# Rows of the weights regrouped by four, chunk 0's key products cut into column halves, and the key weights split on VectorE

## The chip, the cores and the metric

The kernel runs on one core of a Trainium2 chip. TensorE (PE) multiplies matrices; its weight loads are shown apart (PEld). VectorE (DVE), ScalarE (ACT) and GpSimd (POOL) do the elementwise work, and SyncE (SP) issues most of the transfers between HBM and the core's memory (SBUF); a few are issued from ACT's queue. Matrix results land in PSUM. The metric is the device time of one execution in microseconds, as the median of several runs.

## The reference, cut to what matters

All inputs are float32: x is 2048 x 512, wq 512 x 512, wk and wv 512 x 16, w_gate and w_up 512 x 1792, w_down 1792 x 512, gate_w has 512 entries.

```python
g = _sigmoid((x * gate_w).sum(-1, keepdims=True))
# attention: 32 query heads of width 16 share one key and one value head
q = (x @ wq).reshape(B, S, 32, 16)
k = x @ wk
v = x @ wv
p = softmax(einsum(q, k) * 16 ** -0.5)
a = einsum(p, v) @ wo
# feed-forward
b = (silu(x @ w_gate) * (x @ w_up)) @ w_down
return g * a + (1 - g) * b
```

Everything that is multiplied with x sums over the 512 columns of x. In which order these 512 are summed, and in which groups of 128, leaves the result as it is, as long as x and the weights use the same order.

## The kernel before, in words

**Precision.** A product of float32 matrices is made from three products of rounded parts: each operand is split into a high part and the rest (`split`, lines 111 to 114: a cast, L113, and a subtraction, L114), and high by high, high by low and low by high are summed in PSUM.

**Layout.** The 512 columns of x are cut into KD = 4 groups of 128, one group for each of four matrix products. The weights lie in SBUF with a partition p and a group k: before, the row k * 128 + p of a weight matrix lies in partition p, group k. For x the same is made by transposing 128 x 128 squares on PE.

**The start.** The rows of x are worked on in four chunks of 512 rows, each of four tiles of 128 rows. SP fetches the rows of chunk 0 in four transfers and those of the later chunks in two each (`load_x`, L639); chunks share two buffers, so chunk 2 waits until chunk 0 has been transposed. ACT's queue fetches wk, wv and gate_w into one tile `wkv_f` (L643 to L645). `prepare_kv` splits them with eight operations on POOL (L113, L114): wkv_h and wkv_l have 113 columns, which hold the keys three times at two places, the values and the gate.

`transpose_x(c, i)` transposes two row tiles of chunk c: eight PE transposes (L689) into one of two PSUM buffers (`pss`), with the square of x as the loaded weights and the identity streamed through. For chunk 0, KEEP = 6 products of a zero matrix (`zeros`, L675) follow each row tile. Then ACT copies the buffer out as the high part (L693) and DVE subtracts to get the low part (L694), which also sets the buffer free for the next but one `transpose_x`.

`project_kv(c)` makes the 12 products of wkv with chunk c (L123; 512 columns each): eight with the high part of x, four with the low. ACT takes the result out (L709, L711), and POOL makes the rows of `ks` from it (L715, L717). `load_wq(m)` fetches 128 columns of wq (SP, L144) and splits them on POOL.

The engines work each through their own list in the order in which the code is written (`manual_schedule`); the start's order is that of the lines 740 to 786. From line 789 on, jobs for queries, gate, up and down products (L223) are woven between attention scores (L833), exponentials (L844) and value products (L860). Weights w_gate and w_up come through `load_w` and the views `wg_v` and `wu_v`.

Of the kernel before, what the change touches and what calls it, by code (L numbers as in the profile page):

```python
# [18 lines left out]
P = 128  # L19
# [3 lines left out]
DH = 16  # L23
# [19 lines left out]
LONG = 8  # L43
GAP = 36
WARM = 30
KEEP = 6
RATE = 8
FIRST = 6
PTB = 3
# [18 lines left out]
def tile_gated_mix(ctx, tc, x, wq, wk, wv, wo, w_gate, w_up, w_down, gate_w, out):  # L68
# [13 lines left out]
    x_d = dpool.tile([2, 2, P, KD, CH], F32, name="x_d")  # L82
    w_d = dpool.tile([3, NF, 2, P, D], F32, name="w_d")
    o_w = dpool.tile([KD, 2, P, D], F32, name="o_w")
    wq_v = wq.rearrange("(k p) n -> p k n", p=P)

    ident = cpool.tile([P, P], F32, name="ident")
    make_identity(nc, ident)
# [23 lines left out]
    def split(hi, lo, src, eng=nc.gpsimd, eng_hi=nc.vector):  # L112
        eng_hi.tensor_copy(hi, src)  # L113
        eng.tensor_tensor(lo, src, hi.bitcast(F32), ALU.subtract)  # L114
# [8 lines left out]
            nc.tensor.matmul(ps, a, b, start=(i == 0), stop=(i == n - 1))  # L123


    wg_v = w_gate.rearrange("(k p) f -> p k f", p=P)
    wu_v = w_up.rearrange("(k p) f -> p k f", p=P)
    W, HT = {}, {}
    ACTS, DEFER, LOADS, HOLD, EVAC, FRESH = [], [], [], [], [], set()

# [501 lines left out]
    with tc.tile_pool(name="apool", bufs=1) as ap, tc.tile_pool(name="apool2", bufs=2) as a2:  # L632
        XT = {}

        def load_x(c, n):
            XT[c] = a2.tile([P, TC, D], F32, name="xt", bufs=2)
            for i in range(0, TC, n):
                t = c * TC + i
                nc.sync.dma_start(XT[c][:, i:i + n, :], x[t * P:(t + n) * P, :].rearrange("(i p) d -> p i d", p=P))  # L639

        load_x(0, 1)
        wkv_f = ap.tile([P, KD, 2 * DH + 1], F32, name="wkv_f")
        nc.scalar.dma_start(wkv_f[:, :, 0:DH], wk.rearrange("(k p) n -> p k n", p=P))  # L643
        nc.scalar.dma_start(wkv_f[:, :, DH:2 * DH], wv.rearrange("(k p) n -> p k n", p=P))
        nc.scalar.dma_start(wkv_f[:, :, 2 * DH:], gate_w.rearrange("(k p o) -> p k o", p=P, o=1))  # L645
        load_x(1, 2)


        wkv_h = ap.tile([P, KD, KW], F32R, name="wkv_h")
        wkv_l = ap.tile([P, KD, KW], F32R, name="wkv_l")  # L650

        def prepare_kv():
            k, v, g = slice(0, DH), slice(DH, 2 * DH), slice(2 * DH, 2 * DH + 1)
            for r in (0, RT):
                to = [w[:, :, r:r + 3 * DH].rearrange("p k (i n) -> p k i n", i=3) for w in (wkv_h, wkv_l)]
                src = wkv_f[:, :, k].unsqueeze(2).to_broadcast([P, KD, 3, DH])
                split(to[0], to[1], src, nc.gpsimd, nc.gpsimd)
            for to, src in ((3 * DH, v), (KW - 1, g)):
                rows = slice(to, to + src.stop - src.start)
                split(wkv_h[:, :, rows], wkv_l[:, :, rows], wkv_f[:, :, src], nc.gpsimd, nc.gpsimd)  # L660

        spread = ap.tile([DH, DH, HG], F32, name="spread")

        def prepare_norms():
            nc.vector.tensor_reduce(sel, ident.rearrange("p (r h) -> p h r", h=HG), axis=AX.X, op=ALU.max)
            nc.vector.tensor_copy(spread, ident[:DH, :DH].unsqueeze(2).to_broadcast([DH, DH, HG]))
            nc.vector.memset(vaug[:, :, DH:], 1.0)

        nc.gpsimd.memset(ks.bitcast(F32), -1.0)
        nk = ap.tile([DH, NCH + 1], F32, name="nk")  # L670
        VZ = {}

        def zeros(n):
            for i in range(n):
                nc.tensor.matmul(pw[:, :P], warm, warm, start=True, stop=True)  # L675

        def transpose_x(c, i):
            if i == 0:
                if c < 2:
                    new_x(c)  # L680
                else:
                    XC[c] = [PAIR[1].tile([P, S], F32R, name="pt", bufs=PTL).rearrange("p (k s) -> p k s", k=KD)
                             for _ in range(2)]
            xt, (xh, xl) = XT[c], XC[c]
            pt = ps_s.tile([P, 2 * CH], F32, name="pss")
            ptv = pt.rearrange("p (k t) -> p k t", k=KD)
            for j in range(2):
                for k in range(KD):
                    nc.tensor.transpose(ptv[:, k, j * P:(j + 1) * P], xt[:, i + j, k * P:(k + 1) * P], ident)  # L689
                if c == 0:  # L690
                    zeros(KEEP)
            hi = xh[:, :, i * P:(i + 2) * P]
            nc.scalar.activation(hi, ptv, AF.Copy)  # L693
            nc.vector.tensor_tensor(xl[:, :, i * P:(i + 2) * P], ptv, hi.bitcast(F32), ALU.subtract)  # L694

        def store_x(c):
            for j, part in enumerate(XC[c]):
                nc.sync.dma_start(x_d[c - 2, j], part.bitcast(F32))

        def project_kv(c):  # L700
            cs = slice(c * CH, (c + 1) * CH)
            if c % 2 == 0:
                VZ[c // 2] = ap.tile([KW, 2 * CH], F32, name="vz", bufs=2)
            pk = ps_f.tile([P, CH], F32, name="pf")

            terms = [(w[:, k], XC[c][0][:, k]) for k in range(KD) for w in (wkv_h, wkv_l)]
            mm(pk[:KW, :], terms + [(wkv_h[:, k], XC[c][1][:, k]) for k in range(KD)])
            vz = VZ[c // 2][:, c % 2 * CH:(c % 2 + 1) * CH]
            nc.scalar.activation(vz, pk[:KW, :], AF.Copy)  # L709
            ka = a2.tile([DH, CH], F32, name="ka")  # L710
            nc.scalar.activation(ka, pk[:DH, :], AF.Abs)  # L711
            nc.vector.tensor_reduce(nk[:, c:c + 1], ka, axis=AX.X, op=ALU.max)

            for r in (0, RT):
                nc.gpsimd.tensor_copy(ks[r:r + 3 * DH, cs], vz[r:r + 3 * DH, :])  # L715
                lo = slice(r + 2 * DH, r + 3 * DH)
                nc.gpsimd.tensor_tensor(ks[lo, cs], vz[lo, :], ks[lo, cs].bitcast(F32), ALU.subtract)  # L717


        def spread_k():  # L720
            nc.vector.tensor_reduce(nk[:, NCH:], nk[:, :NCH], axis=AX.X, op=ALU.max)
            pn = ps_o.tile([P, CH], F32, name="po")
            nc.tensor.matmul(pn[:, 0:1], spread.rearrange("i r h -> i (r h)"), nk[:, NCH:], start=True, stop=True)  # L723
            nc.vector.tensor_copy(kmax, pn[:, 0:1])

        def transpose_v(b):
            pv = ps_s.tile([P, 2, CH], F32, name="pss")
            for i in range(NT // 2):
                nc.tensor.transpose(pv[:, i // TC, i % TC * KW:(i % TC + 1) * KW], VZ[b][:, i * P:(i + 1) * P],  # L729
                                    ident[:KW, :KW])  # L730
            for j in range(2):
                ts = slice(b * NT // 2 + j * TC, b * NT // 2 + (j + 1) * TC)
                pvb = pv[:, j, :TC * KW].rearrange("p (t n) -> p t n", n=KW)
                nc.vector.tensor_copy(vaug[:, ts, 0:DH], pvb[:, :, 3 * DH:RT])
                nc.scalar.activation(g_sb[:, ts], pvb[:, :, KW - 1], AF.Tanh, scale=0.5)

        with tc.manual_schedule():

            warm = ap.tile([P, P], BF16, name="warm")
            nc.vector.memset(warm, 0.0)  # L740
            pw = ps_o.tile([P, CH], F32, name="po")
            zeros(WARM)
            prepare_kv()
            load_wq(0)
            transpose_x(0, 0)
            transpose_x(0, 2)
            prepare_norms()
            load_x(2, 2)
            transpose_x(1, 0)
            transpose_x(1, 2)  # L750
            load_x(3, 2)
            new_qs(0)
            project_kv(0)
            transpose_x(2, 0)
            transpose_x(2, 2)
            project_kv(1)
            transpose_x(3, 0)
            transpose_x(3, 2)
            project_kv(2)
            store_x(2)  # L760
            transpose_v(0)
            project_kv(3)
            store_x(3)
            load_wq(1)
            load_wq(2)
            load_part()
            for c in range(NCH):
                if c == 2:
                    load_wq(3)
                job = query(0, c)  # L770
                for i in range(job.size):
                    if c == 0 and i == job.size - 1:
                        spread_k()
                    job.step(i)
                if c == 0:
                    transpose_v(1)

                    nc.vector.tensor_scalar(g_sb, g_sb, 0.5, 0.5, op0=ALU.mult, op1=ALU.add)
                    nc.vector.tensor_scalar(c_sb, g_sb, -0.5, 0.5, op0=ALU.mult, op1=ALU.add)
            for nm in "gu":  # L780
                load_w(nm, 0)
            run(STORES, NCH)
            fill(GAP)
            WIDE.append(1)
# [350 lines left out]
```

## Time and profile before

| what | value |
|---|---|
| median of 3 runs | 1311.89 us (1311.57 to 1312.14) |
| the profiled execution's own time | 1310.52 us |
| its span in the profile | 1308.7 us |
| PE busy | 1301.7 us (99%) |
| ACT, DVE, POOL busy | 1077.6, 795.0, 308.5 us |
| start of the first x transposes | 4.17 us |
| start of the first query product | 26.45 us |

Times inside a profile count from the start of the span, and the execution's own time is 1.8 us longer than the span. PE rows are pipelined: a row's duration is longer than the time to the start of the next, so the cost of one product in a stream is the distance between starts.

### The profile page before, as it was taken

What the parts mean: (1) busy time and instruction counts of PE and PEld (TensorE: products, weight loads), DVE (VectorE), ACT (ScalarE), POOL (GpSimd) and SP (SyncE); (2) the same over time, 40 slices, a digit from 0 to 9 for tenths busy, and PEclk for the clock granted to TensorE, in tenths of its full rate; (3) what the DMA queues carried; (4) which work ended last, traced back from release to release, by engine and by line L of the source; (5) the groups of instructions that cost most, each with busy time, mean ns of one, the idle gap of its engine ahead of it and who ended that gap; (6) DMA issues with size and microseconds to landing.
All of it is one profiled execution on the core that took longest, in us unless ns stands there. A gap on an engine that the chain in (4) does not pass through costs nothing.

```text
span 1308.7 us, 27220 instructions
## 1 busy us (share of the span) xinstructions
PE 1301.7 (99%) x10791; PEld 766.1 (59%) x10791; DVE 795.0 (61%) x1210; ACT 1077.6 (82%) x1626; POOL 308.5 (24%) x765
## 2 busy tenths in 40 slices
PE   9999999999999999999999999999999999999998
PEld 7655555555555555555555555555556555555586
DVE  4668665576565665666566566566566666566632
ACT  4588898888888988888889889889898888898710
POOL 7463331442252272273130000000000000001031
PEclk9999999999999999999999999999999999999999
DMA  8674221232233363354134341243242342153075
GB/s 292 210 235 136 81 57 45 67 113 61 69 108 138 127 219 113 109 181 134 62 132 157 120 144 55 71 156 110 85 141 90 119 148 61 62 181 94 25 229 200
DMA packets 104821, 161.57 MB, mean 123 GB/s; under 512 B 12144, under 2 KB 43632, under 8 KB 103024
## 3 DMA queue, kind: packets, MB, share of 16 engines
q1 hardware_dynamic: 102960, 159.56, 37.8%
q8 instruction: 88, 1.44, 0.5%
q10 hardware_dynamic: 1728, 0.20, 0.1%
q14 instruction: 45, 0.37, 0.1%
HBM read 101.52 MB, written 57.67 MB: 122 GB/s over the span
## 4 chain that ended last, share of the span: by engine, by line
PE 99%; DMA 0%; DVE 0%; SPq 0%; ACT 0%; issue 0%
PE pf L223 39%; PE po L860 35%; PE pss L833 20%; PE pf L123 4%; PE pss L689 0%; DMA xt<-in_A_x_dram 0%; PE pss L729 0%; SPq L639 0%; DVE xl L694 0%; ACT xh L693 0%; DVE ot L594 0%; PE po L723 0%; PE po L1047 0%
## 5 line engine op out<-in xcount | busy, mean ns | idle before, releaser
L844 ACT ACTIVATE pt<-pss 128x1024 f32<-128x1024 f32 (+1 forms) x1024 | 776.0, 814 | 148.0 <-PE pss L833 112.8
L839 DVE COPY pt<-pss 128x512 f32<-128x512 f32 x504 | 348.0, 691 | 389.3 <-PE pss L833 382.7
L860 PE MATMUL po<-pt,vaug 128*32 128x512 f32 x4096 | 460.0, 594 | 0.0
L833 PE MATMUL pss<-qs,ks 64*128 64x512 f32 x2048 | 412.7, 406 | 0.0
L833 PEld LDWEIGHTS pss<-qs,ks 64*128 64x128 f32 x2048 | 200.3, 183 | 197.3 <-ACT pt L844 97.1
L860 PEld LDWEIGHTS po<-pt,vaug 128*32 128x32 f32 x4096 | 126.9, 109 | 268.6 <-issue 261.2
L844 ACT ACTIVATE pt<-pt 128x512 f32<-128x512 f32 x504 | 281.4, 629 | 0.0
L223 PE MATMUL pf<-xh,wgh 64*128 64x512 f32 x444 | 161.3, 391 | 0.0
L223 PE MATMUL pf<-xl,wgh 64*128 64x512 f32 x444 | 161.3, 391 | 0.0
L223 PE MATMUL pf<-xh,wgl 64*128 64x512 f32 x444 | 160.5, 391 | 0.0
L223 PE MATMUL pf<-xl,wuh 64*128 64x512 f32 (+1 forms) x444 | 159.5, 391 | 0.0
L223 PE MATMUL pf<-xh,wuh 64*128 64x512 f32 (+1 forms) x444 | 159.4, 392 | 0.0
L223 PE MATMUL pf<-xh,wul 64*128 64x512 f32 (+1 forms) x444 | 158.0, 391 | 0.0
L223 PE MATMUL pf<-wdl,hh 64*128 64x512 f32 (+1 forms) x411 | 143.4, 390 | 0.0
L223 PE MATMUL pf<-wdh,hh 64*128 64x512 f32 (+1 forms) x411 | 143.0, 390 | 0.0
L223 PE MATMUL pf<-wdh,hl 64*128 64x512 f32 (+1 forms) x411 | 143.0, 390 | 0.0
L871 DVE RECIPROCAL rsb<-rsb 128x128 f32<-128x128 f32 x128 | 116.6, 933 | 1.1
L223 PEld LDWEIGHTS pf<-xh,wgh 64*128 64x128 f32 x444 | 76.7, 185 | 5.4
L223 PEld LDWEIGHTS pf<-xl,wgh 64*128 64x128 f32 x444 | 76.7, 185 | 5.4
L223 PEld LDWEIGHTS pf<-xh,wgl 64*128 64x128 f32 x444 | 76.7, 185 | 5.3
L223 PEld LDWEIGHTS pf<-xh,wuh 64*128 64x128 f32 (+1 forms) x444 | 76.0, 185 | 6.3 <-issue 0.8
L223 PEld LDWEIGHTS pf<-xh,wul 64*128 64x128 f32 (+1 forms) x444 | 76.1, 185 | 5.7
(161 smaller groups left out, 1369.6 us busy)
## 6 DMA issues: line engine op xcount, KB each, us to landing
qs<-q_d SPq DMA_DIRECT2D x31, 512.0 KB, 4.9
wraw<-in_B_w_gate_dram SPq DMA_DIRECT2D x28, 256.0 KB, 3.3
wraw<-in_B_w_up_dram SPq DMA_DIRECT2D x28, 256.0 KB, 4.2
q_d<-hh SPq DMA_DIRECT2D x28, 256.0 KB, 3.9
wraw<-in_B_w_down_dram SPq DMA_DIRECT2D x28, 256.0 KB, 3.0
wgh<-w_d SPq DMA_DIRECT2D x28, 256.0 KB, 2.7
wgl<-w_d SPq DMA_DIRECT2D x28, 256.0 KB, 2.9
wuh<-w_d SPq DMA_DIRECT2D x28, 256.0 KB, 2.7
```

Of the source, the lines that this page charges most:

```text
L123: nc.tensor.matmul(ps, a, b, start=(i == 0), stop=(i == n - 1))
L223: ins = nc.tensor.matmul(self.ps, a, b, start=(i == 0 and opens), stop=(last and closes))
L833: nc.tensor.matmul(ps[:, b * CH:(b + 1) * CH], ks[rows, kt * P:(kt + 1) * P], QS[h][rows, j, :], start=True, stop=True)
L839: other = nc.vector.tensor_copy(pt[:, CH:], ps[:, CH:])
L844: ins = nc.scalar.activation(pt[:, w], ps[:, w], AF.Exp, scale=SCALE)
L860: ins = nc.tensor.matmul(po[c * 2 * DH:(c + 1) * 2 * DH, :], vaug[:, kt, :], pt[:, c * CH:(c + 1) * CH], start=(kt == 0), stop=(kt == NT - 1))
L871: nc.vector.reciprocal(rsb[:, w], rsb[:, w])
```

## The change

There are five edits.

1. The views of wq, w_gate, w_up, wk, wv and gate_w put row 4 * p + k into partition p, group k. The transposes of x follow: group k takes the columns k, k + 4, k + 8 and so on, so the square that is loaded as weights is read with a step of four words (16 bytes) instead of one word.
2. The first eight of chunk 0's key products are made in two halves of 256 columns: the half of row tiles 0 and 1 before `transpose_x(1, 0)`, the other before `transpose_x(1, 2)`. The four products with the low part stay whole and come after it.
3. The eight operations of `prepare_kv` run on DVE instead of POOL.
4. KEEP is 2 instead of 6.
5. `load_wq(0)` comes after `load_x(2, 2)` instead of before the transposes of chunk 0.

```diff
-KEEP = 6
+KEEP = 2
...
-    wq_v = wq.rearrange("(k p) n -> p k n", p=P)
+    wq_v = wq.rearrange("(p k) n -> p k n", p=P)
...
-    wg_v = w_gate.rearrange("(k p) f -> p k f", p=P)
-    wu_v = w_up.rearrange("(k p) f -> p k f", p=P)
+    wg_v = w_gate.rearrange("(p k) f -> p k f", p=P)
+    wu_v = w_up.rearrange("(p k) f -> p k f", p=P)
...
-        nc.scalar.dma_start(wkv_f[:, :, 0:DH], wk.rearrange("(k p) n -> p k n", p=P))
+        nc.scalar.dma_start(wkv_f[:, :, 0:DH], wk.rearrange("(p k) n -> p k n", p=P))
...
-                split(to[0], to[1], src, nc.gpsimd, nc.gpsimd)
+                split(to[0], to[1], src, nc.vector, nc.vector)
...
-                    nc.tensor.transpose(ptv[:, k, j * P:(j + 1) * P], xt[:, i + j, k * P:(k + 1) * P], ident)
+                    nc.tensor.transpose(ptv[:, k, j * P:(j + 1) * P], xt[:, i + j].rearrange("t (p k) -> t k p", k=KD)[:, k], ident)
...
+        def key_terms(c, k0, k1, half=None):
+            if c not in PK:
+                PK[c] = ps_f.tile([P, CH], F32, name="pf")
+            cols = slice(0, CH) if half is None else slice(half * 2 * P, (half + 1) * 2 * P)
+            terms = [(w[:, k], XC[c][0][:, k]) for k in range(KD) for w in (wkv_h, wkv_l)]
+            terms += [(wkv_h[:, k], XC[c][1][:, k]) for k in range(KD)]
+            for t in range(k0, k1):
+                nc.tensor.matmul(PK[c][:KW, cols], terms[t][0], terms[t][1][:, cols],
+                                 start=(t == 0 and not half), stop=(t == 3 * KD - 1))
...
             prepare_kv()
-            load_wq(0)
             transpose_x(0, 0)
             transpose_x(0, 2)
             prepare_norms()
             load_x(2, 2)
+            load_wq(0)
+            key_terms(0, 0, 2 * KD, 0)
             transpose_x(1, 0)
+            key_terms(0, 0, 2 * KD, 1)
             transpose_x(1, 2)
             load_x(3, 2)
             new_qs(0)
+            key_terms(0, 2 * KD, 3 * KD)
             project_kv(0)
```

On PE, from the last transposes of chunk 0 to the first of chunk 2, the changed program has these rows (L709 is the product in `key_terms`, which stood at L123; a row of transposes carries its count; the rows between repeat wkv_h and wkv_l):

```order
L689 MATMUL pss<-ident,xt 128x128 x4
L675 LDWEIGHTS warm
L675 MATMUL po<-warm 128x128
L675 LDWEIGHTS warm
L675 MATMUL po<-warm 128x128
L709 MATMUL pf<-xh,wkv_h 113x256
L709 MATMUL pf<-xh,wkv_l 113x256
```

```order
L709 MATMUL pf<-xh,wkv_l 113x256
L689 MATMUL pss<-ident,xt 128x128 x8
L709 MATMUL pf<-xh,wkv_h 113x256
L709 MATMUL pf<-xh,wkv_l 113x256
```

```order
L709 MATMUL pf<-xh,wkv_l 113x256
L689 MATMUL pss<-ident,xt 128x128 x8
L709 MATMUL pf<-xl,wkv_h 113x512 x4
L689 MATMUL pss<-ident,xt 128x128 x16
L709 MATMUL pf<-xh,wkv_h 113x512
```

Eight products of 256 columns now stand ahead of each eight transposes of chunk 1, and only four of 512 columns between them and chunk 2's; before, all twelve stood there.

On SP, at the head of the queue (xt is x, wraw the raw columns of wq; "x4" counts transfers alike):

```order
 L639 DMA xt<-in_A_x_dram 128x512 x4
+L639 DMA xt<-in_A_x_dram 128x2x512 x4
+L144 DMA wraw<-in_A_wq_dram 128x4x128
 L639 DMA xt<-in_A_x_dram 128x2x512 x2
-L144 DMA wraw<-in_A_wq_dram 128x4x128
-L639 DMA xt<-in_A_x_dram 128x2x512 x4
```

The fetch of wq's first columns moved from behind chunk 1 to behind chunk 2.

On DVE, the first rows:

```order
+L113 CAST wkv_h<-wkv_f 128x4x48
+L114 TENSOR_TENSOR wkv_l<-wkv_f,wkv_h 128x4x48
+L113 CAST wkv_h<-wkv_f 128x4x48
+L114 TENSOR_TENSOR wkv_l<-wkv_f,wkv_h 128x4x48
+L113 CAST wkv_h<-wkv_f 128x4x16
+L114 TENSOR_TENSOR wkv_l<-wkv_f,wkv_h 128x4x16
+L113 CAST wkv_h<-wkv_f 128x4
+L114 TENSOR_TENSOR wkv_l<-wkv_f,wkv_h 128x4
 L694 TENSOR_TENSOR xl<-pss,xh 128x4x256 x2
```

The eight split operations stand ahead of the first low part of x (L694) and are gone from POOL.

More of the change, by code (lines that the diff above doesn't have):

```diff
@@ L642, in tile_gated_mix @@
         wkv_f = ap.tile([P, KD, 2 * DH + 1], F32, name="wkv_f")
-        nc.scalar.dma_start(wkv_f[:, :, 0:DH], wk.rearrange("(k p) n -> p k n", p=P))
-        nc.scalar.dma_start(wkv_f[:, :, DH:2 * DH], wv.rearrange("(k p) n -> p k n", p=P))
-        nc.scalar.dma_start(wkv_f[:, :, 2 * DH:], gate_w.rearrange("(k p o) -> p k o", p=P, o=1))
+        nc.scalar.dma_start(wkv_f[:, :, 0:DH], wk.rearrange("(p k) n -> p k n", p=P))
+        nc.scalar.dma_start(wkv_f[:, :, DH:2 * DH], wv.rearrange("(p k) n -> p k n", p=P))
+        nc.scalar.dma_start(wkv_f[:, :, 2 * DH:], gate_w.rearrange("(p k o) -> p k o", p=P, o=1))
         load_x(1, 2)
@@ L656, in prepare_kv @@
                 src = wkv_f[:, :, k].unsqueeze(2).to_broadcast([P, KD, 3, DH])
-                split(to[0], to[1], src, nc.gpsimd, nc.gpsimd)
+                split(to[0], to[1], src, nc.vector, nc.vector)
             for to, src in ((3 * DH, v), (KW - 1, g)):
                 rows = slice(to, to + src.stop - src.start)
-                split(wkv_h[:, :, rows], wkv_l[:, :, rows], wkv_f[:, :, src], nc.gpsimd, nc.gpsimd)
+                split(wkv_h[:, :, rows], wkv_l[:, :, rows], wkv_f[:, :, src], nc.vector, nc.vector)
         spread = ap.tile([DH, DH, HG], F32, name="spread")
@@ L698, in store_x @@
                 nc.sync.dma_start(x_d[c - 2, j], part.bitcast(F32))
+        PK = {}
+        def key_terms(c, k0, k1, half=None):
[7 more added lines that the diff above has]
+                                 start=(t == 0 and not half), stop=(t == 3 * KD - 1))
         def project_kv(c):
@@ L703, in project_kv @@
                 VZ[c // 2] = ap.tile([KW, 2 * CH], F32, name="vz", bufs=2)
-            pk = ps_f.tile([P, CH], F32, name="pf")
-            terms = [(w[:, k], XC[c][0][:, k]) for k in range(KD) for w in (wkv_h, wkv_l)]
-            mm(pk[:KW, :], terms + [(wkv_h[:, k], XC[c][1][:, k]) for k in range(KD)])
+            if c not in PK:
+                key_terms(c, 0, 3 * KD)
+            pk = PK[c]
             vz = VZ[c // 2][:, c % 2 * CH:(c % 2 + 1) * CH]
```

## The prediction

> **What bounds the kernel now.** I read the page's chain of work first, then that chain in order of time over the first 40 us, where nearly all edits lie, and then the timeline of PE there.
>
> ```profile
> PE 99%; DMA 0%; DVE 0%; SPq 0%; ACT 0%; issue 0%
> PEclk9999999999999999999999999999999999999999
> 2.13 4.95 DMA xt<-in_A_x_dram
> 7.13 0.67 PE pss L689 x4
> 7.83 1.03 ACT xh L693
> 8.88 1.24 DVE xl L694
> 10.16 1.09 PE pss L689 x8
> 11.26 2.79 PE pf L123 x12
> 14.05 1.75 PE pss L689 x16
> 15.79 2.77 PE pf L123 x12
> 30.66 9.54 PE pf L223 x42
> ```
>
> PE carries 99% of the chain, at a clock that is never seen throttled. Only up to 10.16 us does the chain leave PE: the fourth row tile of x lands at 7.08, is transposed, copied by ACT, subtracted by DVE, and that frees the PSUM buffer for the second transposes of chunk 1. From there on PE runs without a gap, so what PE saves or loses in the start moves the end by as much, unless a later producer becomes late. PE in the start:
>
> ```profile
> 7.13 0.66 PE L689 MATMUL pss<-ident,xt 128*128 128x128 f32 x4 [0.20 <-DMA xt<-in_A_x_dram]
> 7.63 0.50 PE L675 MATMUL po<-warm 128*128 128x128 bf16 x6
> 8.60 1.06 PE L689 MATMUL pss<-ident,xt 128*128 128x128 f32 x8 [0.47 <-DMA xt<-in_A_x_dram]
> 10.16 1.09 PE L689 MATMUL pss<-ident,xt 128*128 128x128 f32 x8 [0.50 <-DVE xl L694]
> 11.01 0.48 PE L123 MATMUL pf<-xh,wkv_h 128*113 128x512 f32 x1
> 11.56 0.39 PE L123 MATMUL pf<-xh,wkv_h 128*113 128x512 f32 x1
> 11.79 0.40 PE L123 MATMUL pf<-xh,wkv_l 128*113 128x512 f32 x1
> 13.88 1.91 PE L689 MATMUL pss<-ident,xt 128*128 128x128 f32 x16
> 15.55 0.48 PE L123 MATMUL pf<-xh,wkv_h 128*113 128x512 f32 x1
> 20.06 0.48 PE L123 MATMUL pf<-pt,wkv_h 128*113 128x512 f32 x1
> 1300.88 0.28 PE L123 MATMUL pf<-wo0h,xh 128*128 128x256 f32 x1
> 1303.60 0.27 PE L123 MATMUL pf<-wo3h,xl 128*128 128x256 f32 x1
> ```
>
> The bracket is the idle time ahead of a row and what ended it. Some 1.2 us of waiting and the zero products stand where key products could. Costs by distance of starts: a key product of 512 columns 0.23 us (11.56 to 11.79); one of 256 columns 0.118 us (from the end of the kernel: 23 steps in 2.72 us); a transpose 0.107 us (10.16 to 11.01, eight of them); a zero product 0.50 / 6, or 0.083 us.
>
> **The change, part by part.**
>
> *Column halves and KEEP.* Nothing is added but eight more weight loads, hidden in the 0.118 us. Walk PE from 7.13 with the loads at their old price: four transposes 0.42, two zeros 0.17, the first half 8 x 0.118 = 0.95, so 8.67. Chunk 1's first tiles have landed then (8.57), and the high part they need was ready long before. Eight transposes: 9.53. Second half: 10.48; its input is ACT's copy that ends at 8.86. The buffer for the next transposes is free at 10.12, so eight more: 11.34. Four products with the low part: 12.26, where before chunk 2's transposes began at 13.88. That would be 1.6 us, but a new wait takes half of it back. Chunk 2's second eight transposes need the buffer that ACT and DVE empty after 11.34:
>
> ```profile
> L694 DVE TENSOR_TENSOR xl<-pss,xh 128x1024 fp32r<-128x1024 f32 x4 | 4.9, 1225 | 7.1 <-ACT xh L693 7.1
> L693 ACT ACTIVATE xh<-pss 128x1024 fp32r<-128x1024 f32 x4 | 4.1, 1026 | 4.6 <-PE pss L689 4.6
> L278 DVE CAST hh<-hl 128x512 fp32r<-128x512 f32 x1 | 0.4, 426 | 0.1
> L285 DVE TENSOR_TENSOR hl<-pf,hh 128x512 fp32r<-128x512 f32 x4 | 2.8, 688 | 3.5 <-ACT hh L284 2.1 <-ACT hl L284 1.4
> ```
>
> The last transpose drains at about 11.5, ACT ends at 12.55, DVE at 13.83. So PE waits from 13.1 to 13.87, transposes until 14.75 and starts chunk 1's key products there, 15.55 before: **-0.8 us**. Bounds: 0 if another wait stands there, -1.6 without the wait. The chunk 0 key products queue nothing else behind them that anybody needs earlier.
>
> *Split on DVE.* From the last two rows above, 192 columns cost at most 0.43 and 0.69 us, the smaller ones less: about 1.6 us for all eight by length, 4 us at the outside. They need wk, wv and the gate.
>
> ```profile
> 4.17 0.34 POOL L113 CAST wkv_h<-wkv_f 128x192 fp32r<-128x192 f32 x1 [1.14 <-DMA wkv_f<-in_A_wk_dram]
> 10.73 1.09 POOL L113 CAST acc<-wraw 128x512 fp32r<-128x512 f32 x1 [3.55 <-DMA wraw<-in_A_wq_dram]
> 7.82 4.35 SPq L639 DMA_DIRECT2D xt<-in_A_x_dram  x4
> xt<-in_A_x_dram SPq DMA_DIRECT2D x6, 512.0 KB, 5.5
> 33.03 1.55 POOL L114 TENSOR_TENSOR acc<-wraw,acc 128x512 fp32r<-128x512 f32 x1
> 41.17 1.06 POOL L113 CAST acc<-wraw 128x512 fp32r<-128x512 f32 x1 [2.03 <-DMA wraw<-in_A_wq_dram]
> 42.31 1.54 POOL L114 TENSOR_TENSOR acc<-wraw,acc 128x512 fp32r<-128x512 f32 x1
> 33.24 13.76 PE L223 MATMUL pf<-pt,acc 128*128 128x512 f32 x60
> ```
>
> wk is there at 4.17, so DVE is done between 5.8 and 8.2; behind these stand its subtractions, the first at 6.9, and the first key products at 7.7. I take 0, with +0.5 us as the far end.
>
> *wq's first columns later.* The transfer is now issued behind chunk 2's (first issue at 7.82), some 9.2, and at 5.5 us to landing is there near 14.7 instead of 10.73. POOL splits it until about 17.4 (1.09 and 1.54 us), at most 4.0 us later than before; queued behind are the key rows, which no product reads before the scores at 47 (33.24 + 13.76), and the next slices of wq. The first query products come behind the key products of all chunks, past 23 us (chunk 2's begin at 20.06). The second slice was split by 34.6 and is needed at 38.7, the 25th of the 60 products: 4.1 us of slack, and POOL's gaps between the key rows take up most of the delay before that: 0. The tightest one is the last slice: split by 43.85, needed at the 49th of 60 products from 33.24, that is 44.3. It hangs on transfers issued behind PE's own results, so it moves along with PE; POOL sat idle for 2.03 us before it. Chunk 2's x loses 256 KB ahead of it, and lands by some 13.3: in time for 13.87. Cost 0, gain 0.
>
> *Row grouping, transfers.* In HBM the four rows of a partition are neighbours, so wk, wv and gate_w can be read in runs four times as long; in SBUF the pieces stay apart, since `wkv_f` has 33 columns a group. They share the engines with x:
>
> ```profile
> q10 hardware_dynamic: 1584, 0.07, 2.5%
> q1 hardware_dynamic: 128, 0.25, 82.4%
> q1 hardware_dynamic: 212, 0.40, 104.3%
> ```
>
> The first row is their queue over 40 us: 1.0 us of all sixteen engines. The others are x's queue from 5.2 to 6.2 and from 7.2 to 8.2: 0.25 MB in the us that it shares, 0.40 alone. Bounds: nothing, if the pieces decide, to -2.2 us, if x's first MB ran at 0.40 from 2.2 on and landed at 4.9. I take a third of the 1.0 us: **-0.3 us**. The wide weights keep runs of 512 bytes on both sides: 0.
>
> *Row grouping, transposes.* 64 weight loads now step 16 bytes. No row shows PE doing this. The bounds:
>
> ```profile
> L113 POOL CAST acc<-wraw 128x512 fp32r<-128x512 f32 x4 | 4.3, 1072 | 5.6 <-DMA wraw<-in_A_wq_dram 5.6
> L113 POOL CAST wgh<-hh 128x512 fp32r<-128x512 f32 x1 | 0.6, 602 | 0.0
> ```
>
> The same POOL cast takes 1072 ns when it reads with a step of 64 bytes, 602 when it reads in order: 0.92 ns a word more, 0.118 us for 128 words. From below it is 0: a load asks for a word every 0.83 ns (0.107 / 128), while PE's other operand is served every 0.45 ns (0.23 / 512), so reads at half speed would about feed it. This row is of the same engine and memory, the other of another engine at four times the step; I take 0 and hold the other end as the chief rival.
>
> Sum: 1310.52 - 0.8 - 0.3 = 1309.4 for an execution like the profiled one; the median of the runs stands 1.37 above it, so **1310.8**.
>
> **Rivals.** *A: the stepped loads cost 0.118 us each.* For it: the POOL rows, the only stepped reads that can be compared. Against: PE's read rate. PE from 7.13 would need 0.90 + 0.17 + 0.95 + 1.80 + 0.95 + 1.80 + 0.92 = 7.5 us, so chunk 2 starts at 14.6 (+0.7); 16 transposes there and in chunk 3 take 3.6 instead of 1.67 (13.88 to 15.55), +1.9 each: +4.5, less 0.3, gives 1316.1. It decides from +0.07 us a load on, where its sum reaches the bound of a measurable loss. [...]
>
> *B: the start's transfers shrink by the whole 2.2 us.* Then all of the start moves with x's landing: 1311.89 - 0.8 - 2.2 = 1308.9. For it: x's queue runs at 0.25 MB/us beside the small pieces. Against: the pieces in SBUF are unchanged.
>
> *C: the end does not move,* since DVE's late subtraction for chunk 1, or the gate's landing, holds PE until 15.5 anyway: 1311.9. For it: in the walk above DVE already ends last for chunk 2. Against: its work starts at 11.5, not later than before by more than 0.3.
>
> **How the numbers follow.** What a measurement here can tell from no change is about 0.2%, 2.6 us. Forecast 0.52, at 1310.8 with its own range 1309.3 to 1311.8: same. C 0.05: same. A 0.34, with half prices: slower. B 0.09: faster. So faster 0.09, same 0.57, slower 0.34. For the range I go down to B's 1308.9 and up to A's 1316.1 with 0.2 for rounding.
>
> **What would show it.** Right: 16 transposes of chunk 2 or 3 still take 1.9 us and a weight load 141 ns or so; the first key product of chunk 1 begins near 14.5 instead of 15.55; a wait for DVE of about 0.8 us in the middle of chunk 2's transposes; the fourth tile's transposes near 6.8. A shows as 16 transposes in 3.6 us. Wrong in another way would be a PE wait for wkv at the first half, a wait for wq near 25 or 44 us, or a difference that arises after 50 us, where nothing here says one should.

## The result, and the profile after

| | before | after |
|---|---|---|
| median of 22 runs | 1311.45 us | 1313.85 us |
| lowest to highest | 1310.94 to 1312.19 | 1310.81 to 1316.28 |
| the profiled execution | 1310.52 us | 1312.94 us |
| first query product starts | 26.45 us | 28.81 us |

The ratio is 1.0019 (95% interval 1.0013 to 1.0025): 2.4 us slower, where 1.1 us faster was forecast, and the runs spread over 5.5 us instead of 1.3. The two profiled executions differ by 2.42 us, and the first query product (the first row of L223) by 2.36 us: all of it arises in the first 29 us. The forecast stood on the 1311.89 us of three runs; 22 runs put the kernel before 0.44 us lower. In the comparisons further down, one run of the kernel before took 1619.23 us and is left out.

First the chain of waits of the changed kernel, in order of time. The columns are start, length and what the chain passes through.

```profile
1.65 5.77 DMA xt<-in_A_x_dram
7.46 1.12 PE pss L689 x4
8.59 0.21 PE po L675 x2
8.80 0.85 PE pss L689 x4
9.92 1.55 PE pf L709 x8
11.46 0.96 PE pss L689 x8
12.43 0.95 PE pf L709 x8
13.38 0.97 PE pss L689 x8
14.37 1.03 ACT xh L693
15.43 1.24 DVE xl L694
16.71 1.23 PE pss L689 x8
17.95 2.77 PE pf L709 x12
```

The last five rows are the wait that the prediction had named: chunk 2's second transposes wait for ACT and DVE. It stands at 16.71 and not at 13.87. The delay is older: the third tile of x, which before was transposed at 5.99, lands at 7.42, and PE needs until 9.87 for two tiles of transposes and four zero products. The rows of PE, DVE and POOL show why. Before:

```profile
5.99 0.61 PE L689 MATMUL pss<-ident,xt 128*128 128x128 f32 x4
6.11 0.24 POOL L113 CAST wkv_h<-wkv_f 128x64 fp32r<-128x64 f32 x1
6.70 0.19 POOL L113 CAST wkv_h<-wkv_f 128x4 fp32r<-128x4 f32 x1
6.91 1.23 DVE L694 TENSOR_TENSOR xl<-pss,xh 128x1024 fp32r<-128x1024 f32 x1 [5.97 <-ACT xh L693]
```

After:

```profile
5.30 0.28 PE L675 MATMUL po<-warm 128*128 128x128 bf16 x2
7.46 1.12 PE L689 MATMUL pss<-ident,xt 128*128 128x128 f32 x4 [1.89 <-DMA xt<-in_A_x_dram]
8.60 1.06 PE L689 MATMUL pss<-ident,xt 128*128 128x128 f32 x4
9.92 0.53 PE L709 MATMUL pf<-xh,wkv_h 128*113 128x256 f32 x1
7.27 0.20 DVE L113 CAST wkv_h<-wkv_f 128x64 fp32r<-128x64 f32 x1 [1.52 <-DMA wkv_f<-in_A_wv_dram]
9.60 0.17 DVE L113 CAST wkv_h<-wkv_f 128x4 fp32r<-128x4 f32 x1 [1.87 <-DMA wkv_f<-in_gate_w_dram]
9.88 2.35 DVE L694 TENSOR_TENSOR xl<-pss,xh 128x1024 fp32r<-128x1024 f32 x2
```

The split of wv (64 columns over the four groups) starts at 7.27 and that of gate_w (4) at 9.60; before, POOL started them at 6.11 and 6.70. DVE, which now waits for them in front of its work on x, begins the first subtraction at 9.88 instead of 6.91. And PE ran slowly. By windows (length; busy time and count of PE, PEld, DVE, ACT and POOL; then the granted clock, the DMA share and GB/s):

```profile
6.00:7.00 1.00, 0.00 (x0) 0.00 (x0) 0.00 (x0) 0.53 (x1) 0.00 (x0) 1.00 1.01 298
7.00:8.00 1.00, 0.54 (x3) 0.54 (x4) 0.42 (x2) 0.00 (x0) 0.00 (x0) 0.65 1.05 400
8.00:9.00 1.00, 1.00 (x7) 0.93 (x6) 0.00 (x0) 0.00 (x0) 0.00 (x0) 0.50 0.87 334
9.00:10.00 1.00, 0.95 (x7) 0.65 (x5) 0.37 (x3) 0.31 (x1) 0.00 (x0) 0.50 0.22 82
10.00:11.00 1.00, 1.00 (x6) 1.00 (x7) 1.00 (x1) 0.72 (x1) 0.00 (x0) 0.64 0.37 53
11.00:12.00 1.00, 1.00 (x10) 1.00 (x9) 1.00 (x2) 0.00 (x0) 0.00 (x0) 1.00 0.89 225
```

The clock is 0.50 from about 7.3 (0.65 in the us from 7) to about 10.7 (0.64 in the us from 10). Before, no fall is recorded in the start. But a clock of 1.00 at the very beginning says nothing: the profile's clock records begin only some us into the span (at 4.70 before, at 3.89 after, between 3.76 and 7.03 in the 18 profiles of this document), and the views show 1.00 where there is no record. PE was slow ahead of them. In the kernel before, four transposes that began ahead of the first record, at 4.17, took 0.86 us, and four behind it, at 5.21, 0.61. In the last kernel of the experiments the records begin at 6.86, and four transposes take as long ahead of it as in the fall above (1.06 us at 8.60):

```profile
4.17 1.06 PE L689 MATMUL pss<-ident,xt 128*128 128x128 f32 x4
5.67 1.06 PE L689 MATMUL pss<-ident,xt 128*128 128x128 f32 x4
7.02 0.61 PE L689 MATMUL pss<-ident,xt 128*128 128x128 f32 x4
```

So each execution has some luck in its first us, and one profile against one other can't settle a few tenths of a us.

There were three suspects for the loss: late transfers, a gate that DVE and PE now wait for, and the clock; beside them the stepped weight loads. The tile view gives these:

```profile
L689 PEld LDWEIGHTS pss<-ident,xt x64: 195/211/226, 4.0 to 22.2; 128*128 128x128 f32 x64
L689 PEld LDWEIGHTS pss<-ident,xt x64: 138/141/230, 4.1 to 19.9; 128*128 128x128 f32 x64
```

The first row is after, the second before (minimum, median and maximum in ns). One load takes 70 ns more. But in a stream of sixteen they start every 0.127 us (20.32 to 22.36) where it was 0.117 (18.17 to 20.04), since loads overlap: that is 0.01 us each, not 0.118.

### The profile page after: what moved, and what is told of

It reads as the page before. It is cut to its first block, busy times and chain, and to the rows that moved or that the text cites. A ratio compares the mean times of both kernels' runs of the same rounds, so it can differ in the third digit from the quotient of the medians.

```text
span 1311.2 us, 27203 instructions
## 1 busy us (share of the span) xinstructions
PE 1302.8 (99%) x10783; PEld 766.0 (58%) x10783; DVE 795.1 (61%) x1218; ACT 1077.5 (82%) x1626; POOL 308.7 (24%) x757
## 4 chain that ended last, share of the span: by engine, by line
PE 99%; DMA 0%; DVE 0%; ACT 0%; SPq 0%; issue 0%
PE pf L223 39%; PE po L874 35%; PE pss L847 20%; PE pf L123 3%; PE pf L709 1%; PE pss L689 1%; DMA xt<-in_A_x_dram 0%; PE pss L740 0%; DVE xl L694 0%; ACT xh L693 0%; SPq L639 0%; DVE ot L594 0%; PE po L675 0%; PE po L734 0%; PE po L1061 0%
## 5 line engine op out<-in xcount | busy, mean ns | idle before, releaser
L223 PE MATMUL pf<-xh,wgh 64*128 64x512 f32 x444 | 161.3, 391 | 0.0
L223 PE MATMUL pf<-xl,wgh 64*128 64x512 f32 x444 | 161.0, 391 | 0.0
L223 PE MATMUL pf<-xh,wgl 64*128 64x512 f32 x444 | 160.5, 391 | 0.0
L223 PE MATMUL pf<-xh,wuh 64*128 64x512 f32 (+1 forms) x444 | 159.5, 392 | 0.0
L223 PE MATMUL pf<-xl,wuh 64*128 64x512 f32 (+1 forms) x444 | 159.4, 391 | 0.0
L223 PE MATMUL pf<-xh,wul 64*128 64x512 f32 (+1 forms) x444 | 157.9, 391 | 0.0
L223 PE MATMUL pf<-wdl,hh 64*128 64x512 f32 (+1 forms) x411 | 143.3, 390 | 0.0
L223 PE MATMUL pf<-wdh,hh 64*128 64x512 f32 (+1 forms) x411 | 142.8, 390 | 0.0
L223 PE MATMUL pf<-wdh,hl 64*128 64x512 f32 (+1 forms) x411 | 142.8, 390 | 0.0
L223 PEld LDWEIGHTS pf<-xh,wgl 64*128 64x128 f32 x444 | 76.7, 185 | 5.8
L223 PEld LDWEIGHTS pf<-xh,wgh 64*128 64x128 f32 x444 | 76.7, 185 | 5.7
L223 PEld LDWEIGHTS pf<-xl,wgh 64*128 64x128 f32 x444 | 76.6, 185 | 5.7
L223 PEld LDWEIGHTS pf<-xh,wuh 64*128 64x128 f32 (+1 forms) x444 | 76.0, 185 | 6.1 <-issue 0.8
L223 PEld LDWEIGHTS pf<-xh,wul 64*128 64x128 f32 (+1 forms) x444 | 76.0, 185 | 5.4
```

The source lines that it names most:

```text
L223: ins = nc.tensor.matmul(self.ps, a, b, start=(i == 0 and opens), stop=(last and closes))
```

## The experiments

Each kernel ran beside the kernel before on the same chip. Medians are of 11 runs (8 for the last three that change rows alone); those of before are of 32 or 33 and lie between 1311.07 and 1311.41.

**KEEP back to six.**

```diff
-KEEP = 2
+KEEP = 6
```

> The change with KEEP back at 6. Theory 'clock': the granted TensorE clock fell to 0.50 from about 7.5 to 10.7 us because PE sat idle from 5.5 to 7.46, and how long it stays down differs from run to run; with six zero products a tile the clock stays at 1.00 through the start, the runs lie within about 1.3 us of each other as those of the kernel before do, and the median falls by 1 to 2 us to 1312 to 1313. Rival 'transfers': the start is late because wk, wv, gate_w and the third tile of x land late (4.5, 7.2, 9.6 and 7.4 us); then the median stays near 1313.9 and the clock makes no difference.

Measured: 1312.66, ratio 1.0008 (0.9999 to 1.0017). Its clock shows no fall in the start, yet the first query product starts at 28.97, no earlier than in the change's own profile. Its rows:

```profile
9.79 0.17 DVE L113 CAST wkv_h<-wkv_f 128x4 fp32r<-128x4 f32 x1 [1.62 <-DMA wkv_f<-in_gate_w_dram]
10.10 0.34 PE L709 MATMUL pf<-xh,wkv_h 128*113 128x256 f32 x1 [1.28 <-DVE wkv_h L113]
```

With PE at full speed the gate ends last: PE waits 1.28 us for it at the first half of key products, and DVE's subtractions wait behind it. So the median fell by 1.2 us, into the range of the clock theory, though the two intervals against the kernel before overlap; and the spread did not close (1310.5 to 1316.3). The clock is one part, and in a profile where its fall is gone the gate takes its place.

**Rows back.** Weights and transposes as before, all else as in the change.

```diff
-    wq_v = wq.rearrange("(p k) n -> p k n", p=P)
+    wq_v = wq.rearrange("(k p) n -> p k n", p=P)
...
-xt[:, i + j].rearrange("t (p k) -> t k p", k=KD)[:, k]
+xt[:, i + j, k * P:(k + 1) * P]
```

> The change without the row grouping (weights and transposes as before; halves, KEEP 2, split on VectorE and the later wq transfer stay). Theory 'transfers': wv and gate_w land by 5.2 and 6.1 us and the third tile by 6.0 as before, VectorE's first subtraction starts by 7, and the walk of the prediction holds: 1310.4 to 1311.0, PE clock 1.00. Rival 'clock': KEEP 2 is enough to let the clock fall, 1312 or more with runs 3 to 5 us apart. Rival 'stepped loads': their price was the loss; then 16 transposes take 1.9 us again and the gain is 64 x 0.01 = 0.8 us only.

Measured: 1310.67, ratio 0.9993 (0.9984 to 1.0002), 3.2 us below the change. The row grouping is necessary for the loss. The median is where the prediction's walk had it, though the interval does not exclude no change. In its profile gate_w is split at 7.09 and the first subtraction starts at 7.38, not at 6.9; and one transfer of chunk 3, now behind wq, landed at 19.36 and held PE, so that profile's first query product, at 26.70, is no earlier than before.

**Split on POOL again.**

```diff
-split(to[0], to[1], src, nc.vector, nc.vector)
+split(to[0], to[1], src, nc.gpsimd, nc.gpsimd)
```

> The change with the key weights split on GpSimd again. Theory 'gate ahead of x on VectorE': the two small operations that wait for gate_w until 9.6 us hold the subtractions of x behind them; without them the first starts near 6.6 instead of 9.9 and the second follows its copy by ACT, worth 1 to 1.5 us: 1312.4 to 1312.9, with the spread of the clock still there. Rival: PE's first half of key products waits for the same gate, so nothing is gained: 1313.9.

Measured: 1311.75, ratio 1.0004 (0.9995 to 1.0013), better than expected. DVE's first subtraction starts at 6.55. The profiled execution took the longest of the eleven (1315.28), and its clock fell:

```profile
10.47 0.19 POOL L113 CAST wkv_h<-wkv_f 128x4 fp32r<-128x4 f32 x1 [2.12 <-DMA wkv_f<-in_gate_w_dram]
7.00:8.00 1.00, 0.73 (x4) 0.73 (x5) 0.78 (x1) 0.00 (x0) 0.24 (x1) 0.72 1.05 388
10.00:11.00 1.00, 0.29 (x1) 0.27 (x2) 0.47 (x1) 0.49 (x1) 0.40 (x2) 0.50 0.21 51
13.00:14.00 1.00, 1.00 (x7) 1.00 (x6) 0.00 (x0) 0.00 (x0) 0.00 (x0) 0.50 1.03 387
14.00:15.00 1.00, 1.00 (x9) 1.00 (x8) 0.00 (x0) 0.49 (x1) 0.00 (x0) 0.86 0.85 267
```

The clock is down from about 7.4 to 14.3, twice as long as in the change's profile: PE waits again, for gate_w at 10.47, while it is low. The first query product starts at 30.85.

**Rows alone.** The kernel before with the row grouping only.

```diff
-    wq_v = wq.rearrange("(k p) n -> p k n", p=P)
+    wq_v = wq.rearrange("(p k) n -> p k n", p=P)
...
-xt[:, i + j, k * P:(k + 1) * P]
+xt[:, i + j].rearrange("t (p k) -> t k p", k=KD)[:, k]
```

> The kernel before with the row grouping alone (KEEP 6, split on GpSimd, whole products, wq early). Theory 'transfers': wv and gate_w land near 7.2 and 9.6 and the third tile near 7.4 here too, so it is slower than before by 1.5 to 2.5 us, 1313 to 1314, with the clock at 1.00. Rival 'stepped loads' alone: transfers land as before and it costs 0.5 to 0.8 us, 1312.0 to 1312.3. Rival 'order of the transfers': they land as before and the time is unchanged.

Measured: 1312.15, ratio 1.0006 (0.9997 to 1.0015): not told from no change, and less than expected. The landings are those of the change (gate_w split at 9.60, third tile at 7.46), and the clock shows no fall. The whole key products come only after chunk 1's transposes here (12.4), so the late gate holds nobody; the late x does, and in this profile the first query product starts at 28.25. By the medians grouping alone makes 0.7 of the 2.4 us.

**KEEP 2 alone,** in the kernel before.

```diff
-KEEP = 6
+KEEP = 2
```

> The kernel before with KEEP 2 alone. Theory 'two together': the clock falls only when few zero products meet the late third tile; with the transfers as before PE is never idle for more than about 1 us here, the clock stays at 1.00 in the start, the end does not move because the fourth tile's landing and VectorE set it: 1311.2 to 1311.6. Rival 'KEEP 2 is enough': the clock shows 0.50 for some us in the profile or the runs spread over 3 us, 1312 or more.

Measured: 1312.44, ratio 1.0007 (0.9998 to 1.0016), unclear, with no fall of the clock in the profile. The expected 1311.2 to 1311.6 was not met. In its profiled execution (1312.95) the fourth tile landed late and the first query product starts at 27.18, 0.7 later than before. Another 1.0 us arises at 46.20, where PE waits for POOL's split of wq's last columns: on SP's queue a transfer ahead of their fetch took 1.73 us to issue (at 38.17) instead of 0.54. The rest arises between 92 and 114 us. None of this is seen to come from KEEP.

**Halves alone,** and **halves with wq behind chunk 2.** Both with the old rows, KEEP 6 and the split on POOL.

```diff
+            key_terms(0, 0, 2 * KD, 0)
             transpose_x(1, 0)
+            key_terms(0, 0, 2 * KD, 1)
             transpose_x(1, 2)
...
+            key_terms(0, 2 * KD, 3 * KD)
             project_kv(0)
```

> The kernel before with the column halves alone (old row order, KEEP 6, split on GpSimd, wq fetched early). The prediction's walk: a gain of 0.8 us, 1310.4 to 1310.8, with a wait for VectorE in the middle of chunk 2's transposes. Rival: another wait takes its place (x of chunk 2 or 3 landing late, as one tile of chunk 3 did at 19.4 us with wq moved): 1311.2 to 1311.6.

```diff
             prepare_kv()
-            load_wq(0)
...
             load_x(2, 2)
+            load_wq(0)
```

> The kernel before with the column halves and wq's first columns behind chunk 2 (old row order, KEEP 6, split on GpSimd): the candidate to beat both. Theory: nothing on VectorE waits for the gate, chunk 2's x lands 0.7 us earlier than with wq ahead of it, so the 0.7 us wait for it goes; 1310.2 to 1310.7, below 1311.4 of the kernel before. Rival: chunk 3's x, now behind wq, lands at 19 and holds its second transposes as with the rows put back: 1310.7 to 1311.3.

Measured: 1311.30, ratio 0.9998 (0.9989 to 1.0007), and 1311.12, ratio 0.9999 (0.9990 to 1.0008). With wq early, chunk 2's first transposes waited 0.74 us for x, the rival; with wq late they did not, and the wait for DVE is where the prediction put it:

```profile
12.70 1.04 PE L689 MATMUL pss<-ident,xt 128*128 128x128 f32 x8
14.31 1.09 PE L689 MATMUL pss<-ident,xt 128*128 128x128 f32 x8 [0.57 <-DVE xl L694]
```

The first query product starts at 26.07, 0.38 us earlier than before, one execution against one. The medians show no gain (1310.2 to 1310.7 was expected with wq late), but their intervals don't exclude 0.8 us either.

**Stepped loads alone,** and **grouped weights alone.** Each leaves x and the weights in different orders.

```diff
-xt[:, i + j, k * P:(k + 1) * P]
+xt[:, i + j].rearrange("t (p k) -> t k p", k=KD)[:, k]
```

> The kernel before with the step of 16 bytes in the transposes alone; the weights keep the old row order, so the columns of x meet the wrong rows and the products are not the reference's (nothing is left out). Transfers as before. Theory 'stepped loads cost little': 16 transposes take 1.92 us instead of 1.75, 0.011 us each, of which about 40 lie on the chain: plus 0.4, 1311.7 to 1311.9, third tile at 6.0, gate_w at 6.1. Rival A of the prediction would be plus 4 us.

```diff
-    wq_v = wq.rearrange("(k p) n -> p k n", p=P)
+    wq_v = wq.rearrange("(p k) n -> p k n", p=P)
...
```

> The kernel before with the weights' rows grouped alone; the transposes read in order, so again the products are not the reference's (nothing is left out). Theory 'transfers': gate_w lands at 9.5 or later, the third tile near 7.4, plus 0.3 to 0.7 us: 1311.7 to 1312.1. Rival: the landings are as before and the late ones came from the stepped reads or from the moved wq.

Measured: 1311.54, ratio 1.0002 (0.9993 to 1.0011), and 1311.22, ratio 0.9999 (0.9990 to 1.0008). The stepped loads leave the landings alone (third tile at 5.76, gate_w split at 7.02) and sixteen transposes on the chain take 1.92 us. The grouped weights bring the late landings (wv 7.95, gate_w 10.89, third tile 7.52), and in this order of work cost nothing that can be measured. Both came out below what was expected.

**The same two, undone in the change.**

```diff
-xt[:, i + j].rearrange("t (p k) -> t k p", k=KD)[:, k]
+xt[:, i + j, k * P:(k + 1) * P]
```

> The change with the transposes reading in order again; the weights' rows stay grouped, so the products are not the reference's (nothing is left out). Theory 'late small transfers': gate_w still lands at 9.5 or later, VectorE's first subtraction still waits for it, the clock still falls to 0.50 in most runs: 1313.0 to 1313.8. Rival 'stepped loads': near 1311, clock 1.00.

```diff
-    wq_v = wq.rearrange("(p k) n -> p k n", p=P)
+    wq_v = wq.rearrange("(k p) n -> p k n", p=P)
...
```

> The change with the weights' rows in the old order; the transposes still read with a step of 16 bytes, so the products are not the reference's (nothing is left out). Theory 'late small transfers': gate_w lands by 7.2, the clock stays at 0.999 or 1.00 in all runs, and only the loads' 0.4 to 0.7 us stand against the kernel with both undone: 1311.0 to 1311.4. Rival 'stepped loads': 1313 or more.

Measured: with the steps taken back 1312.79, ratio 1.0013 (1.0004 to 1.0022); with the weights' rows back 1311.12, ratio 0.9999 (0.9990 to 1.0009) and all runs between 1310.4 and 1311.5. The first lies just under its range, and 5 of its 11 runs show the low mean clock (0.998 or less) that no run of the second does. So it is the weights' rows, not the step. The first one's rows show the whole sequence once more:

```profile
10.69 0.17 DVE L113 CAST wkv_h<-wkv_f 128x4 fp32r<-128x4 f32 x1 [2.18 <-DMA wkv_f<-in_gate_w_dram]
11.01 0.53 PE L709 MATMUL pf<-xh,wkv_h 128*113 128x256 f32 x1 [2.15 <-DVE wkv_h L113]
10.00:11.00 1.00, 0.00 (x0) 0.02 (x1) 0.28 (x3) 0.00 (x0) 0.00 (x0) 0.79 0.96 248
13.00:14.00 1.00, 1.00 (x7) 1.00 (x6) 1.00 (x4) 0.00 (x0) 0.00 (x0) 0.50 0.99 320
14.00:15.00 1.00, 1.00 (x11) 1.00 (x10) 0.01 (x1) 0.53 (x1) 0.02 (x1) 1.00 0.15 44
```

Here PE idled for 1.67 us behind x (5.33 to 6.99) and the clock stayed up; it falls at 10.59, while PE idles for the gate, for 3.4 us.

**KEEP 6 and the split on POOL, rows grouped.**

```diff
-KEEP = 2
+KEEP = 6
...
-split(to[0], to[1], src, nc.vector, nc.vector)
+split(to[0], to[1], src, nc.gpsimd, nc.gpsimd)
```

> The change with KEEP 6 and the split on GpSimd, row grouping kept. Theory: with neither the clock's fall nor the gate ahead of x on VectorE only the stepped loads and the late x are left, less what the halves gain; but PE's first half of key products waits for the gate until about 10: 1311.3 to 1312.2, no run below a clock of 0.999. Rival: the two are one loss, and it equals the better of the two alone (1311.75).

Measured: 1311.74, ratio 1.0008 (0.9999 to 1.0017), no run below a clock of 0.999. It equals the split on POOL alone, as the rival had it. PE's first half of key products starts at 10.53 behind a gate split at 10.29.

**Which rows.** Only wk, wv and gate_w; only the wide weights; only gate_w, each in the kernel before. The lines that are grouped:

```diff
+wk.rearrange("(p k) n -> p k n", p=P), wv.rearrange("(p k) n -> p k n", p=P), gate_w.rearrange("(p k o) -> p k o", p=P, o=1)
...
+wq.rearrange("(p k) n -> p k n", p=P), w_gate.rearrange("(p k) f -> p k f", p=P), w_up.rearrange("(p k) f -> p k f", p=P)
...
+gate_w.rearrange("(p k o) -> p k o", p=P, o=1)
```

> The kernel before with the rows of wk, wv and gate_w alone grouped (the products are not the reference's; nothing is left out). Theory 'the small transfers delay themselves': their issues on ACT's queue take 0.64 us instead of 0.53, wv is split at 7.2 or later, gate_w at 9.5 or later, the third tile starts near 7.4. Rival 'wide transfers': wv by 6.1, gate_w by 7.5, third tile by 6.5.

> The kernel before with the rows of wq, w_gate and w_up alone grouped (the products are not the reference's; nothing is left out). Theory 'the small transfers delay themselves': wv is split by 6.1, gate_w by 7.5, third tile by 6.5 as before, and the time is that of the kernel before, 1310.3 to 1312.5. Rival: the late landings of the change appear here.

> The kernel before with the rows of gate_w alone grouped (the gate is not the reference's; nothing is left out). If each grouped transfer is slower by itself, gate_w alone is late (8 or later) with wv at 6.1; if wk and wv in the queue ahead of it are what makes it late, it comes by 7.5.

Measured: 1311.41, 1311.68 and 1311.43, ratios 1.0003, 1.0003 and 1.0004, each with an interval of 0.0010 to both sides that takes in no change. gate_w is split at 7.90, 7.81 and 9.51. The wide weights alone leave wv at 6.04 and the third tile at 6.46, as before. gate_w alone is late by itself. But the three small ones together gave 7.90, against 9.60 to 10.89 in all seven profiles with every weight grouped: wv at 6.71 and the third tile at 7.02, and not the late gate that was expected. Each of these is a single profile. The issues on ACT's queue take 0.64 to 0.66 us where the rows are grouped, 0.46 to 0.53 where not.

**Without rows, KEEP 6.** The change with the old row order, and:

```diff
-KEEP = 2
+KEEP = 6
```

> The change without the row grouping and with KEEP 6: halves, split on VectorE, wq behind chunk 2. Theory: with the gate at 7.5 the first subtraction starts at 7.4 instead of 6.9, the clock stays, and it is like the same kernel with KEEP 2: 1310.3 to 1311.0, at most 0.7 below the kernel before, so a clear win is not expected. Rival: KEEP 6 costs the start 0.3 us more than KEEP 2.

Measured: 1311.33, ratio 1.0001 (0.9992 to 1.0010). That is above the expected 1310.3 to 1311.0. No version of these clearly beats the kernel before; the lowest is the change with the rows put back.

**The clock, over all runs.** A fall of 3.4 us at half speed takes 0.0013 off an execution's mean clock (an estimate: half of 3.4 in 1311). The 15 profiles without a fall after the records begin lie between 0.9988 and 1.000. Runs with a mean clock of 0.998 or less:

| | weights' rows old | weights' rows grouped |
|---|---|---|
| KEEP 6 | 0 of 44 | 0 of 44 |
| KEEP 2 | 0 of 33 | 20 of 44 |

The kernel before beside them had none in 131. The four cells hold, from the top left: the two halves kernels, the stepped loads alone and the last one; KEEP back, rows alone, grouped weights alone, and KEEP 6 with POOL; rows back, KEEP 2 alone and weights back; the change (12 of 22), the split on POOL (3 of 11) and the steps back (5 of 11). Of the change's own runs, the 12 have a median of 1315.1, the other 10 of 1312.9. The count is a lower bound: a single fall of 3.4 us can still round to 0.999, as in the change's profiled execution (0.9987). The mean is also lowered by a varying amount after PE's last product: in the profile of the kernel before the clock reads 0.51 in the last 0.16 us of the span, in the change's 1.00 to its end. Of the 44 with KEEP 6 and grouped rows, 24 show 1.000, which leaves no room for a fall.

## Why the prediction was wrong, step by step

**What bounds the kernel:** right. The end moved by what the start lost: 2.36 us at the first query product, 2.42 at the end. "At a clock that is never seen throttled" held of the records, which begin at 4.70 us there, and no longer held once PE idled (0.50 from 7.31 in the change, behind 1.73 us of idling). "From there on PE runs without a gap" is also luck in part: the last slice of wq, which the prediction called the tightest, held PE at 46.20 in the profile of KEEP 2 alone.

**Column halves and KEEP (-0.8 us):** the mechanism was right, and the wait behind DVE came where it was put. So were the lengths: from the first half to chunk 1's first key product the walk has 7.03 us (7.72 to 14.75), and with the old rows 7.11 (8.20 to 15.31, rows back) and 7.09 (8.07 to 15.16, halves with wq behind chunk 2) were taken. Too early was the start, which hangs on the fourth tile (7.13 in the walk; 7.62 with the rows back, where it had to be waited for). But the step missed a need. The gate is the last of the 113 columns, so the first half of key products needs gate_w some three us sooner than the whole products did. "The chunk 0 key products queue nothing else behind them" was wrong: chunk 1's transposes stand behind them on PE, and waited for the gate (1.28 us with KEEP 6, 2.15 with the steps back). This is the "PE wait for wkv at the first half" that the prediction had listed as a sign of being wrong.

**KEEP:** its zero products were counted as time saved and no more. With the rows grouped, they were what kept the clock up through a late tile: 0 of 44 runs have a mean clock of 0.998 or less, against 20 of 44.

**Split on VectorE (0, at most +0.5):** failed. It reckoned from the landing of wk (4.17) alone. The eight operations last 2.0 us in sum, near the 1.6 forecast, but the last two pairs wait for wv and gate_w, and the subtractions of x stand behind. Putting them on POOL is worth 2.1 us in the change's median (1311.75 against 1313.85, not run side by side; the intervals against the kernel before touch at 1.0013). With KEEP 6 it is 0.9 us, not told from nothing.

**Row grouping, transfers (-0.3):** the step that failed most. Bounds from 0 to -2.2 left no room for a loss, without a reason. The runs of four times the length that it counted on never reached the queue, which moves the same 1584 packets in both kernels, none longer than 64 bytes. Instead the small transfers came later: gate_w is split at 9.5 or later in eight of nine profiles that group its rows, at 7.81 or earlier in the nine that do not. PE waits for the third tile of x until 6.87 to 7.94 in the seven profiles with every weight grouped; in the nine with gate_w's rows old it starts on it at 5.73 to 7.10 without a wait. With the weights' rows put back, the 2.4 us are gone (1311.12).

**Row grouping, transposes (0):** nearly right: 0.01 us a load. **Rival A is refuted:** from the first of 16 transposes to the product behind them 1.84 us pass (20.55 to 22.39), where A had 3.6 and the kernel before 1.67. The load itself went from 141 to 211 ns; what it costs PE is 0.01 us, since the next load starts 0.127 us behind it and runs beside it. Rival B went the other way. C had a chance of 0.05 and named the gate's landing as what might hold PE. PE did wait for it in four profiles (0.64 to 2.15 us), but C put the cost at nothing.

**The later wq** cost nothing by itself, but put chunk 3's x behind it, which in one profile held PE at 19.36.

So the walk to 14.75 became 17.70. By the change's profile, from the walk's 7.72 for the start of the first half: the third and fourth tile, landed together, need PE until about 8.8 even at full clock (+1.0); the half clock adds 1.1 there and 0.4 in the first half (9.92 to 11.30 instead of 0.95); the steps some 0.4 in all up to 17.70. That is 2.9 of the 2.95. It is the account of one execution: in others, as in the profile of KEEP 6, the gate takes the clock's place.

**What stays open:** why grouped rows land later, since the queue moves the same 1584 packets of the same bytes; why the three small ones alone delayed the gate less than gate_w alone; whether KEEP 2 alone costs anything, since the interval does not tell its 1.3 us from nothing; and what decides when the clock's records begin in an execution.

## What to carry to other kernels

When work is moved forward, list every operand that it needs and ask when each lands, the smallest ones too: a 2 KB vector held up two engines here. Filler products on PE are priced by the wait that they might have to cover, not by the wait in the profile at hand. And a changed access pattern of a transfer can go either way: its bound includes a loss until a run of the same pattern is seen. In a profile, look where the clock's records begin before reading 1.00 as full speed.

## What the runs showed of the hardware

- In three profiles the granted clock fell to 0.50 after PE had idled for 1.7 us (5.58 to 7.31 in the change, 8.87 to 10.59 with the steps taken back; with the split on POOL at 7.45, behind 1.70 us of idling), and stayed there for 3.4 us (the first two) or 6.8 us (the split on POOL). Idling of 1.67 us (the steps taken back, 5.33 to 6.99) did not make it fall. From the beginning of the records to a fall it is 3.41 us (from 3.89 in the change) or 6.83 (with the steps taken back).
- Ahead of the clock's first record PE was slow: in the last kernel, with records from 6.86 on, four transposes take 1.06 us ahead of it and 0.61 behind it; in the kernel before, with records from 4.70 on, 0.86 (at 4.17) and 0.61 (at 5.21).
- Weight loads of 128 words with a step of 16 bytes last 211 ns instead of 141, and in a stream start every 0.127 us instead of every 0.117.
- Grouping four neighbouring rows a partition lengthened each small transfer's issue from 0.46 to 0.53 us to 0.64 to 0.66 us, with the same packets, and moved gate_w's split from 7.81 at the latest to 9.5 and more in eight of nine profiles.
